# Chunked attention and a rational-activation feed-forward layer on one core: token blocks of 256 in place of 384, 256-column matmuls, attention in quarters, and an instruction order written out by hand

## The chip, the cores and the metric

The kernel runs on one core of a Trainium2 chip. The metric is the device time of one execution in microseconds (us), as the median of several executions. The core's engines each work through their own list of instructions, in order, and wait for one another on semaphores: TensorE (PE in the profile; PEld is its weight load), VectorE (DVE), ScalarE (ACT), GpSimd (POOL) and SyncE (SP), which here issues the DMAs. Matmuls write to PSUM, eight banks of 512 float32 columns; everything else lies in SBUF.

## The reference

Two stages, one behind the other. First attention inside chunks of 64 tokens: 8 batches, 8 heads, 576 tokens, head size 64, so 9 chunks for each head. Then a feed-forward layer over all 4608 tokens (d_model 512, d_ff 2048) with a rational function between its two matrices.

```
scores = scale * np.matmul(q_c, k_c.transpose(0, 1, 2, 4, 3))      # 64x64 per chunk and head
attn = np.exp(scores - np.max(scores, axis=-1, keepdims=True))
attn = attn / (np.sum(attn, axis=-1, keepdims=True) + 1e-09)
x = np.matmul(attn, v_c)                                          # then (4608, 512), heads side by side
h = x @ w_in                                                      # w_in 512 x 2048, float64
P = a[0] + a[1] * h + a[2] * h2 + a[3] * h3                       # h2 = h*h, h3 = h2*h
Q = 1.0 + np.abs(b[0]) * np.abs(h) + np.abs(b[1]) * h2
out = (P / (Q + 1e-6)) @ w_out                                    # w_out 2048 x 512, float64
```

The weights come as float64 and are rewritten to float32 on the chip. Both big products are made in three matmuls each, since the factors are split into a rounded part (hi) and a rest (lo): hi*hi, hi*lo and lo*hi.

## The kernel before

**Blocks and steps.** The 4608 tokens are cut into 12 blocks of 384 (`BT`), each of three units of 128 tokens. A block goes through d_ff in 8 steps of 256 (two slices of 128). A step is: the first product, FF1 (`ff1_mm`, L252): two slices of 12 matmuls of 384 columns, into one pair of PSUM banks `ph`, of which there is one; a chain of elementwise operations; and the second product, FF2 (`ff2_mm`, L334), which runs two steps later (`LAG`): 18 matmuls of 512 columns into three banks `po0` to `po2`, which gather over the 8 steps of a block. So a block has 192 FF1 matmuls of 384 columns and 144 FF2 matmuls of 512.

**The chain.** ACT copies `ph` to `h` in SBUF (L281), then makes A=|b0 h| (L282), B=h^2 (L283) and C=a3 h+a2 (L284) from `h`. DVE makes Q in B (L293) and the numerator in C (L294, L295). ACT makes 1/Q as exp(-ln Q) in A (L288, L289). DVE makes `ghi` (L303) and the rest `glo` (L304 to L306). All work on 128 x 768 values.

**Attention.** One unit is 128 tokens of all heads. `att_s` (S below) makes the scores with 8 matmuls whose moving operand `kbd` holds two chunks' keys in a block-diagonal form with zeros, so 64 stationary and 128 moving columns over all 128 rows (L172). DVE takes the maximum (L183), ACT the exponentials with their sums (L187, 8 instructions with a read of the accumulator each), DVE divides. `att_t` (T) transposes (L205), ACT copies the two halves to the block-diagonal `abd` (L208). `att_av` (AV) multiplies with v (L226), ACT and DVE split the result into `xhi` and `xlo` (L233, L238). The operands are float32, and the trace shows each such matmul as two, while a transposition is one. The units of the next block are spread over the steps of the present one.

**Weights.** 32 pieces of 128 x 512 are loaded and decoded (DVE L122, L124, L125, ACT L123, L126); the rest of a piece is made on DVE (L134) or, for half of the pieces, on TensorE with two products into PSUM (L130, L131) and a copy by ACT (L132).

**What sets the order.** The source is written step by step, and a planner with a model of the instructions' times orders each engine's list; only the last two steps are kept as they are written. `PROLOGUE` says what stands before the first FF1, and `DECODED` how many pieces are decoded by which step.

Of the kernel before, what the change touches and what calls it, by code (L numbers as in the profile page):

```python
# [38 lines left out]
def tile_chunked_attention_rational_moe(  # L39
# [30 lines left out]
    loaded = {}  # L70

    def load(u, qt=None, kt=None, vt=None, part="qkv"):
        if u >= NU:
            return
        if qt is None:
            qt = p2.tile([P, 512], F32, tag="qt", name=f"qt{u}", bufs=1)
            vt = p2.tile([P, 512], F32, tag="vt", name=f"vt{u}", bufs=1)
            kt = kbd
        loaded[u] = (qt, kt, vt)
        if "q" in part:  # L80
            load_qk(u)
        if "v" in part:
            load_v(u)

    def load_qk(u):
        qt, kt, vt = loaded[u]
        nc.sync.dma_start(out=qt, in_=qT[u])
        for par in range(2):
            rows = slice(64 * par, 64 * par + 64)
            nc.sync.dma_start(out=kt[rows, par, :], in_=kT[u, rows, :])  # L90

    def load_v(u):
        nc.sync.dma_start(out=loaded[u][2], in_=vP[u])

    def zero_rest(kt):
        nc.gpsimd.memset(kt[0:64, 1, :], 0.0)
        nc.gpsimd.memset(kt[64:128, 0, :], 0.0)

    def load_early(u):
        flat = lambda t: t.rearrange("p a b -> p (a b)")  # L100
        kt = p2.tile([P, NHP, BT], F32, tag=("xhi", "xlo")[u % 2], name=f"kt{u}")
        kt = flat(kt)[:, :1024].rearrange("p (a b) -> p a b", a=2)
        qt = p2.tile([P, 2, BT], F32, tag="A", name=f"qt{u}")
        vt = p2.tile([P, 2, BT], F32, tag="B", name=f"vt{u}")
        zero_rest(kt)
        load(u, flat(qt)[:, :512], kt, flat(vt)[:, :512], "q")
# [4 lines left out]
    raws = {}  # L111

    def piece_load(i, src):
        raw = p2.tile([P, 512, 2], I32, tag="raw", name=f"raw{i}", bufs=4)
        nc.sync.dma_start(out=raw, in_=src.rearrange("p (f w) -> p f w", w=2))
        raws[i] = raw

    def piece_decode(i, hi, lo):
        raw = raws.pop(i)
        low, high = raw[:, :, 0], raw[:, :, 1]  # L120
        val = high.bitcast(F32)
        nc.vector.tensor_scalar(low, low, 29, None, ALU.logical_shift_right)  # L122
        nc.scalar.activation(val, val, AF.Copy, scale=2.0 ** -111)  # L123
        nc.vector.scalar_tensor_tensor(low, high, 3, low, ALU.logical_shift_left, ALU.bitwise_or)  # L124
        nc.vector.scalar_tensor_tensor(high, high, -(2 ** 31), low, ALU.bitwise_and, ALU.bitwise_or)  # L125
        nc.scalar.activation(hi, val, AF.Copy, scale=2.0 ** -8)  # L126
        if i in LO_ON_PE:
            tag = ("pss", "pst", "psx")[i % 3]
            pl = ps_a.tile([P, 512], F32, tag=tag, name="pl")
            nc.tensor.matmul(pl, ident, val, start=True, stop=False)  # L130
            nc.tensor.matmul(pl, nident, hi, start=False, stop=True)  # L131
            nc.scalar.activation(lo, pl, AF.Copy, scale=2.0 ** -8)  # L132
        else:
            nc.vector.scalar_tensor_tensor(lo, val, 2.0 ** -8, hi.bitcast(F32), ALU.mult, ALU.subtract)  # L134

    def w_in_piece(fq, cc):
        f = slice(512 * fq, 512 * fq + 512)
        words = slice(1024 * fq, 1024 * fq + 1024)
        return w_in[cc * P:(cc + 1) * P, words], wi_hi[:, cc, f], wi_lo[:, cc, f]

    def w_out_piece(fc):
        return w_out[fc * P:(fc + 1) * P, :], wo_hi[:, fc, :], wo_lo[:, fc, :]

    make_identity(nc, ident)
    nident = cp.tile([P, P], F32R, tag="nident", name="nident")
    nc.vector.tensor_scalar_mul(nident, ident, -256.0)
    nc.gpsimd.memset(abd[0:64, 1, :], 0.0)
# [13 lines left out]
    ebuf = {}  # L161

    def att_s(u):
        qt, kt, vt = loaded[u]
        if u < UPB:
            pss = ps_o.tile([P, 512], F32, tag=f"po{u}", name=f"pss{u}")
        else:
            pss = ps_a.tile([P, 512], F32, tag="pss", name=f"pss{u}")
        for hp in range(NHP):
            for j in range(2):  # L170
                c0 = hp * 128 + j * 64
                nc.tensor.matmul(  # L172
                    pss[j * 64:(j + 1) * 64, hp * 128:(hp + 1) * 128],
                    qt[:, c0:c0 + 64],
                    kt[:, :, c0:c0 + 64],
                    start=True, stop=True,
                )
# [293 lines left out]
```

## Time and profile before

| | us |
|---|---|
| median of 3 executions | 974.58 (974.03 to 974.93) |
| span of the profiled execution, first to last instruction | 971.9 |
| what lies around the span, by that median | 2.7 |
| TensorE busy in it | 942.6 (97%) |
| weight loads busy | 816.3 (84%) |
| VectorE busy | 787.5 (81%) |
| ScalarE busy | 702.0 (72%) |
| first FF1 matmul starts at | 37.7 |

The profile is of one execution. A row of a timeline gives start and duration in us, the engine, the line of the source and the operation with its operands (what is written, an arrow, what is read: of a matmul first the moving, then the stationary operand), then shapes and a count. "128*64" is rows times columns of the array in use. A row of a group gives a count, the busy time, the mean duration in ns of one, and the idle time before them. Matmuls overlap in their pipeline, so the distance from one start to the next, and not the duration, tells what one costs in a stream.

### The profile page before, as it was taken

Reading aid. Unit: us, or ns where it says so; the run is one execution under the profiler, and the core shown is the slowest. Engines: PE = TensorE matmul, PEld = TensorE weight load, DVE = VectorE, ACT = ScalarE, POOL = GpSimd, SP = SyncE. Lnnn points to the kernel's source line nnn. Section 1 sums busy time; section 2 is a strip of 40 time slices with the busy share of each in tenths; the row PEclk is TensorE's granted clock in tenths of the full one; section 3 lists DMA queues with packets and bytes.
Section 4 is the critical chain, followed back from the end, with each engine's and each line's share of the span. In section 5 each row is a group of like instructions: output and inputs, shape, how many; then the busy total and the mean of one; then the engine's idle time right before and its main releaser. Section 6 shows DMA issues by size and latency. Waiting matters only on the chain.

```text
span 971.9 us, 14009 instructions
## 1 busy us (share of the span) xinstructions
PE 942.6 (97%) x5376; PEld 816.3 (84%) x5376; DVE 787.5 (81%) x1011; ACT 702.0 (72%) x1353; POOL 4.9 (1%) x16
## 2 busy tenths in 40 slices
PE   4599999999999999999999999999999999999998
PEld 3477788898888888888888888888888888888996
DVE  6799999878787887887887887877877878877786
ACT  4799889758667777667767767775876776775764
POOL 2000000000000000000000000000000000000000
PEclk9799999999999999999999999999999999999999
DMA  7644423002002112101101100110111211100000
GB/s 252 189 154 142 163 87 110 12 1 66 4 30 66 33 33 65 34 12 59 61 12 52 56 24 26 62 44 23 65 33 34 65 33 34 65 12 1 33 1 33
DMA packets 26274, 55.43 MB, mean 57 GB/s; under 512 B 3680, under 2 KB 3680, under 8 KB 26208
## 3 DMA queue, kind: packets, MB, share of 16 engines
q1 hardware_dynamic: 26208, 54.54, 17.7%
q8 instruction: 42, 0.69, 0.3%
q14 instruction: 24, 0.20, 0.1%
HBM read 45.09 MB, written 9.44 MB: 56 GB/s over the span
## 4 chain that ended last, share of the span: by engine, by line
PE 89%; DVE 4%; DMA 3%; ACT 3%; issue 1%; SPq 1%; DVEq 0%; ACTq 0%
PE po L334 40%; PE ph L252 39%; PE pss L172 4%; PE psx L226 3%; DMA raw<-in_w_in 2%; PE pst L205 1%; DMA raw<-in_w_out 1%; PE pl L130 1%; ACT e L187 1%; DVE raw L124 1%; ACT raw L123 0%; DVE raw L125 0%; DVE raw L122 0%; SPq L90 0%; DVE C L295 0%
## 5 line engine op out<-in xcount | busy, mean ns | idle before, releaser
L252 PE MATMUL ph<-xhi,wi_hi 128*128 128x384 f32 x760 | 260.0, 342 | 3.7 <-ACT h L281 3.0
L252 PE MATMUL ph<-xlo,wi_hi 128*128 128x384 f32 x760 | 256.9, 338 | 0.2 <-DVE xlo L238 0.2
L252 PE MATMUL ph<-xhi,wi_lo 128*128 128x384 f32 x760 | 256.6, 338 | 0.0
L334 PE MATMUL po<-wo_hi,ghi 128*128 128x512 f32 x570 | 227.3, 404 | 0.0
L334 PE MATMUL po<-wo_lo,ghi 128*128 128x512 f32 x570 | 222.8, 396 | 0.0
L281 ACT COPY h<-ph 128x768 f32<-128x768 f32 x95 | 76.1, 802 | 202.1 <-PE ph L252 199.3
L252 PEld LDWEIGHTS ph<-xhi,wi_hi 128*128 128x128 f32 x760 | 143.3, 189 | 14.1 <-ACT h L281 4.4
L293 DVE SCALAR_TENSOR_TENSOR B<-B,ab,A 128x768 f32<-128x768 f32 x95 | 96.6, 1017 | 67.7 <-ACT B L283 67.1
L334 PE MATMUL po<-wo_hi,glo 128*128 128x512 f32 x570 | 150.4, 397 | 0.0
L252 PEld LDWEIGHTS ph<-xlo,wi_hi 128*128 128x128 f32 x760 | 143.4, 189 | 3.9 <-DVE xlo L238 0.7
L252 PEld LDWEIGHTS ph<-xhi,wi_lo 128*128 128x128 f32 x760 | 143.4, 189 | 0.8 <-issue 0.5
L334 PEld LDWEIGHTS po<-wo_hi,ghi 128*128 128x128 f32 x570 | 107.0, 188 | 27.0 <-issue 5.3
L303 DVE SCALAR_TENSOR_TENSOR ghi<-C,ab,A 128x768 fp32r<-128x768 f32 x94 | 95.7, 1018 | 41.7 <-ACT A L289 35.6
L334 PEld LDWEIGHTS po<-wo_hi,glo 128*128 128x128 f32 x570 | 106.7, 188 | 26.3 <-issue 0.8
L334 PEld LDWEIGHTS po<-wo_lo,ghi 128*128 128x128 f32 x570 | 107.0, 188 | 21.5 <-issue 1.6
L288 ACT ACTIVATE A<-B,cst 128x768 f32<-128x768 f32 x95 | 89.6, 943 | 13.4 <-DVE B L293 13.0
L305 DVE SCALAR_TENSOR_TENSOR B<-C,ab,B 128x768 f32<-128x768 f32 x95 | 96.8, 1019 | 2.5
L295 DVE SCALAR_TENSOR_TENSOR C<-C,ab,h 128x768 f32<-128x768 f32 x95 | 96.6, 1017 | 1.9
L284 ACT ACTIVATE C<-h,ab 128x768 f32<-128x768 f32 x95 | 96.6, 1017 | 0.1
L306 DVE TENSOR_TENSOR glo<-B,A 128x768 fp32r<-128x768 f32 x94 | 89.9, 956 | 5.4
L294 DVE TENSOR_TENSOR C<-C,h 128x768 f32<-128x768 f32 x95 | 90.4, 952 | 3.8 <-ACT C L284 3.8
L304 DVE SCALAR_TENSOR_TENSOR B<-B,ghi 128x768 f32<-128x768 f32 x94 | 90.0, 957 | 2.5
(95 smaller groups left out, 993.4 us busy)
## 6 DMA issues: line engine op xcount, KB each, us to landing
qt<-in_qT SPq DMA_DIRECT2D x36, 256.0 KB, 2.9
vt<-in_vP SPq DMA_DIRECT2D x36, 256.0 KB, 2.8
out<-o SPq DMA_DIRECT2D x36, 256.0 KB, 2.2
kbd<-in_kT SPq DMA_DIRECT2D x68, 128.0 KB, 3.3
raw<-in_w_in SPq DMA_DIRECT2D x16, 512.0 KB, 4.8
raw<-in_w_out SPq DMA_DIRECT2D x16, 512.0 KB, 3.7
kt<-in_kT SPq DMA_DIRECT2D x4, 128.0 KB, 4.7
ab<-in_a SPq DMA_DIRECT2D x1, 2.0 KB, 2.5
```

Source lines behind the costliest of these rows:

```text
L252: nc.tensor.matmul(acc, w, x[:, cc, :], start=(k == 0), stop=(k == 11))
L281: yield nc.scalar.copy(h, ph[:, :, :BT])
L284: yield nc.scalar.activation(C, h, AF.Identity, bias=a2, scale=a3)
L288: nc.scalar.activation(A, B, AF.Ln, bias=cst[:, 0:1], scale=2.0 ** -KLN)
L293: yield nc.vector.scalar_tensor_tensor(B, B, b1a, A, ALU.mult, ALU.add)
L294: yield nc.vector.tensor_mul(C, C, h)
L295: yield nc.vector.scalar_tensor_tensor(C, C, a1, h, ALU.add, ALU.mult)
L303: yield nc.vector.scalar_tensor_tensor(ghi, C, a0, A, ALU.add, ALU.mult)
L304: yield nc.vector.scalar_tensor_tensor(B, B, CQ, ghi.bitcast(F32), ALU.add, ALU.mult)
L305: yield nc.vector.scalar_tensor_tensor(B, C, a0, B, ALU.add, ALU.subtract)
L306: yield nc.vector.tensor_mul(glo, B, A)
L334: nc.tensor.matmul(obuf[n][i], g[:, fi, i * 128:(i + 1) * 128], w[:, 2 * s + fi, :], start=(s == 0 and k == first[i]), stop=(s == NST - 1 ...
```

## The change

Nearly the whole body is rewritten; what is computed stays the same.

- **Sizes.** 18 blocks of 256 tokens. A block goes through d_ff in 4 steps of 512 (`FPS`, four slices). FF1 (`ff1`, L281) is 48 matmuls of 256 columns for each step. FF2 (`ff2`, L346) has 24 products for each step, each issued as two matmuls of 256 columns with the same weights, but for the first and the last one into a bank of a block, which stay at 512: two for each of a block's first and last step. The elementwise work is on 128 x 1024 values, 72 steps in place of 96.
- **PSUM.** Four pairs of banks: `p0` and `p1`, which FF1 uses in turns (after the first ten steps), `po` for FF2, `pa` for attention and the weights' rests. The copy `h` is gone: ACT makes A, B, C straight from PSUM (L287, L290, L294), and DVE reads it there too (L310, L314).
- **Attention** is made a block (256 tokens) at a time, in three stages at the block's steps 0, 1 and 2. `quarters` (L178) makes scores and the product with v from 64 x 64 pieces, 32 for each, which take the four quarters of the array in turn: the row half goes with the chunk and the column half with the batch of rows that is written, and the two row halves write to different banks. No block-diagonal copies and no zeros are left, and q, k and v come in loads of 128 x 1024.
- **Weights** come as 16 pieces of 2 x 128 x 512; the rest of 9 of them is made on TensorE (L163, L164), of 7 on DVE (L156).
- **Order.** `tc.manual_schedule()` keeps each engine's list as the source has it. The first 12 steps follow a string, `START`, in which each letter is an operation of one engine and the number a step, a piece or a block; the first two blocks take turns there, step by step, so that each group of weights serves two steps. From step 12 a loop writes the order out.
- **End.** The last two steps are no longer cut in halves.

```diff
-UPB = 3          # units of a token block
+UPB = 2
+FPS = 4
+START = (
+    "q0 w0 S0 v0 k0 M0 w1 U0 s0 o0 E0 j0 q1 n0 s1 o1 N0 w2 j1 T0 i0 K0 v1 i1 A0 h0 h1 r0 o2 X0 s2 Y0 r1 w3 l0 j2 "
+    "S1 i2 l1 w4 h2 M1 F0 s3 o3 U1 E1 j3 i3 o4 s4 r2 n1 N1 a0 j4 c0 w5 i4 b0 p0 l2 h4 Q0 T1 h3 d4 s5 o5 w6 P0 K1 "
...
+    def quarters(out_cols, tile_out, stat, mov):
+        for g in range(NQ):
+            for par in range(2):
+                for c in range(2):
+                    rows = slice(64 * c, 64 * c + 64)
+                    cols = slice(g * 128 + par * 64, g * 128 + par * 64 + 64)
+                    nc.tensor.matmul(
+                        tile_out[par * 64:(par + 1) * 64, c, out_cols(g)],
+                        stat[rows, cols], mov[rows, cols], start=True, stop=True,
+                    )
...
+        ph = bank_pair(tag, f"ph{n}_{s}").rearrange("p a (b t) -> p (a b) t", t=BT)
+        for fi in range(FPS):
+            f = slice((FPS * s + fi) * P, (FPS * s + fi + 1) * P)
...
+            for k, (w, x, cc) in enumerate(mm):
+                nc.tensor.matmul(ph[:, fi, :], w[:, cc, f], x[:, cc, :], start=(k == 0), stop=(k == len(mm) - 1))
...
-        yield nc.scalar.copy(h, ph[:, :, :BT])
-        yield nc.scalar.activation(A, h, AF.Abs, scale=b0)
+        nc.scalar.activation(ch[n, s][1], ch[n, s][0], AF.Abs, scale=b0)
...
+        mm = [(ghi, w, fi, i) for fi in range(FPS) for i in range(2) for w in (wo_hi, wo_lo)]
+        mm += [(glo, wo_hi, fi, i) for i in range(2) for fi in range(FPS)]
...
+            start, stop = s == 0 and k == first[i], s == NST - 1 and k == last[i]
+            for c in ([slice(0, DM)] if start or stop else [slice(0, 256), slice(256, DM)]):
+                nc.tensor.matmul(
+                    obuf[n][:, i, c], g[:, fi, i * 128:(i + 1) * 128], w[:, FPS * s + fi, c], start=start, stop=stop,
+                )
...
+    for g in range(FIRST, total + LAG):
+        n, s = steps[min(g, total - 1)]
+        m, stage = n + 1, s if n + 1 < NB and g < total else None
...
+        if g < total:
+            one("Fab", g)
+            if stage == 1:
+                one("nN", m)
+            one("cQ", g)
+            if stage == 0:
+                one("SMU", m)
+                load_qk(m + 1)
+            if stage == 2:
+                one("A", m)
+                load_v(m + 1)
+            one("IJpP", g)
+            if stage == 0:
+                one("E", m)
+            if stage == 2:
+                one("X", m)
+            one("gHRG", g)
+            if stage == 2:
+                one("Y", m)
+        back = steps[g - LAG]
+        one("Z", g - LAG)
+        if back[1] == NST - 1:
+            store(back[0], last=(back[0] == NB - 1))
+        if stage == 1:
+            one("TK", m)
```

In these strings F is FF1 and Z is FF2; a, b, c are ACT's A, B, C and I, J its ln and exp; Q, p, P, g, H, R, G are DVE's seven operations in the order L298, L310, L314, L319, L323, L327, L331. S, T, A are the three matmul groups of attention, M, U, n, N its DVE operations, E the exponentials, K, X, Y the copies and the rest. Of the weights, w loads, o, j, i are DVE's and s, h ACT's decoding, r is the rest on TensorE and l its copy, d the rest on DVE. q and v load, O stores.

On TensorE, in the middle of the program before: the end of FF2 of step 3, a transposition, FF1 of step 6 and, inside FF2 of step 4, the AV of a unit (`pst` and `psx` are attention's banks, `po` FF2's, the number behind `ph` and `ghi` is the step).

```order
L334 MATMUL po_2_4017<-wo_hi,glo_3_4139 128x512 x2
L205 MATMUL pst_4270<-ident,e_4176 128x128 x4
L334 MATMUL po_0_4015<-wo_hi,ghi_4_4241 128x512
L252 MATMUL ph_6_4277<-xhi_3318,wi_hi 128x384
L252 MATMUL ph_6_4277<-xlo_3319,wi_hi 128x384
...
L334 MATMUL po_0_4015<-wo_lo,ghi_4_4241 128x512
L334 MATMUL po_1_4016<-wo_hi,ghi_4_4241 128x512
L334 MATMUL po_1_4016<-wo_lo,ghi_4_4241 128x512
L226 MATMUL psx_4321<-abd,vt_4161 64x128 x8
L334 MATMUL po_2_4017<-wo_hi,ghi_4_4241 128x512
```

The same engine in the middle of the program after: the end of a block's FF2 (step 3), the transpositions of the next block, FF1 of step 2, the AV, FF2 of the next block's step 0 and FF1 of step 3.

```order
L346 MATMUL po_4075<-wo_hi,glo_3_4183 128x256 x6
L346 MATMUL po_4075<-wo_hi,glo_3_4183 128x512
L238 MATMUL pst_4527<-ident,e_4335 128x128 x8
L281 MATMUL ph_2_4538<-xhi_4065,wi_hi 128x256
L281 MATMUL ph_2_4538<-xlo_4066,wi_hi 128x256
...
L178 MATMUL psx_4594<-at_4536,v_4059 64x64 x32
L346 MATMUL po_4643<-wo_hi,ghi_0_4352 128x512
L346 MATMUL po_4643<-wo_lo,ghi_0_4352 128x256 x2
...
L346 MATMUL po_4643<-wo_hi,glo_0_4353 128x256 x16
L281 MATMUL ph_3_4690<-xhi_4065,wi_hi 128x256
```

FF1 and FF2 now follow each other whole, attention stands between them and no longer inside, and a block has one group each of scores, transpositions and AV, where 256 tokens had two of each.

On VectorE, the first instructions before (`raw` are pieces of weights, `sm` the maxima and sums, `pss` scores, `e` the exponentials):

```order
L183 TENSOR_REDUCE sm_137<-pss_128 128x8
L192 TENSOR_TENSOR e_138<-pss_128,sm_137 128x512
L122 TENSOR_SCALAR raw_108<-raw_108 128x512
L124 SCALAR_TENSOR_TENSOR raw_108<-raw_108 128x512
L183 TENSOR_REDUCE sm_155<-pss_146 128x8
L194 TENSOR_REDUCE sm_137<-e_138 128x8
L125 SCALAR_TENSOR_TENSOR raw_108<-raw_108 128x512
L192 TENSOR_TENSOR e_156<-pss_146,sm_155 128x512
```

And after, up to the rest of the first block's x, which FF1 reads:

```order
L204 TENSOR_TENSOR e_130<-pss_88,sm_126 128x2x8x64
L137 TENSOR_SCALAR raw_86<-raw_86 128x1024
L145 SCALAR_TENSOR_TENSOR raw_86<-raw_86 128x1024
L226 TENSOR_REDUCE sm_126<-e_130 128x16
...
L137 TENSOR_SCALAR raw_128<-raw_128 128x1024
L232 TENSOR_TENSOR e_130<-e_130,sm_126 128x2x8x64
L145 SCALAR_TENSOR_TENSOR raw_128<-raw_128 128x1024
L149 SCALAR_TENSOR_TENSOR raw_86<-raw_86 128x1024
L149 SCALAR_TENSOR_TENSOR raw_128<-raw_128 128x1024
L137 TENSOR_SCALAR raw_146<-raw_146 128x1024
L267 TENSOR_TENSOR xlo_206<-psx_164,xhi_205 128x2x4x128
```

Before the first FF1 there now stands one block of 256 tokens and two pieces of 1024 columns; before, it was three units and four pieces of 512, with parts of later ones between.

More of the change, by code (lines that the diff above doesn't have):

```diff
@@ L65, in tile_chunked_attention_rational_moe @@
     ident = cp.tile([P, P], F32, tag="ident", name="ident")
-    kbd = cp.tile([P, 2, 512], F32, tag="kbd", name="kbd")
-    abd = cp.tile([P, 2, 512], F32, tag="abd", name="abd")
+    nident = cp.tile([P, P], F32R, tag="nident", name="nident")
     ab = cp.tile([P, 8], F32, tag="ab", name="ab")
[L70 to L106, printed above, removed]
@@ L111, in tile_chunked_attention_rational_moe @@
[L111 to L147, printed above, removed]
@@ new lines, in load_v, with w_in_pieces, w_out_pieces @@
+    def load_v(n):
+        if n >= NB:
+            return
+        v = p2.tile([P, W], F32, tag="vt", name=f"v{n}")
+        nc.sync.dma_start(out=v, in_=vP[n])
+        loaded["v", n] = v
+    def w_in_pieces(fq):
+        f = slice(512 * fq, 512 * fq + 512)
+        words = slice(1024 * fq, 1024 * fq + 1024)
+        return [(w_in[c * P:(c + 2) * P, words], wi_hi[:, c:c + 2, f], wi_lo[:, c:c + 2, f]) for c in (0, 2)]
+    def w_out_pieces(fq):
+        return [(w_out[c * P:(c + 2) * P, :], wo_hi[:, c:c + 2, :], wo_lo[:, c:c + 2, :]) for c in (4 * fq, 4 * fq + 2)]
@@ L333, in ff2_mm @@
         for k, (g, w, fi, i) in enumerate(mm):
-            nc.tensor.matmul(
-                obuf[n][i], g[:, fi, i * 128:(i + 1) * 128], w[:, 2 * s + fi, :],
-                start=(s == 0 and k == first[i]), stop=(s == NST - 1 and k == last[i]),
-            )
-    def store(n):
-        for i in range(UPB):
-            o = p2.tile([P, DM], F32, tag="o", name=f"o{n}_{i}")
-            nc.scalar.copy(o, obuf[n][i])
-            r0 = n * BT + i * 128
-            nc.sync.dma_start(out=out[r0:r0 + 128, :], in_=o)
@@ new lines, in tile_chunked_attention_rational_moe, with ph_tag, po_tag, consts @@
+    steps = [(n, s) for s in range(NST) for n in (0, 1)] + [(n, s) for n in range(2, NB) for s in range(NST)]
+    def ph_tag(g):
+        return "p1" if g == 1 or (g >= 10 and g % 2 == 0) else "p0"
+    def po_tag(n):
+        return "p1" if n == 1 else "po"
+    make_identity(nc, ident)
+    nc.gpsimd.memset(cst[:, 0:1], CQ * 2.0 ** -KLN)
+    nc.gpsimd.memset(cst[:, 1:2], -KLN * math.log(2.0))
+    nc.vector.tensor_scalar_mul(nident, ident, -256.0)
+    def consts(_):
+        nc.sync.dma_start(out=ab[:, 0:4], in_=a.partition_broadcast(P))
+        nc.sync.dma_start(out=ab[:, 4:6], in_=b.partition_broadcast(P))
+        nc.scalar.activation(b1a, ab[:, 5:6], AF.Abs)
```

450 lines of the change are left out of this document (204 added, 246 removed), and 9 rows, old and new, of the table START.

## Prediction

> **What bounds the kernel now.** First the page: busy shares, the slices, the chain that ended last.
>
> ```profile
> PE 942.6 (97%) x5376; PEld 816.3 (84%) x5376; DVE 787.5 (81%) x1011; ACT 702.0 (72%) x1353; POOL 4.9 (1%) x16
> ...
> PE   4599999999999999999999999999999999999998
> ...
> PE 89%; DVE 4%; DMA 3%; ACT 3%; issue 1%; SPq 1%; DVEq 0%; ACTq 0%
> ```
>
> TensorE is full from the third slice (some 48 us) to the end, and 89% of the chain is its own. A busy PE need not be at its peak, so the second look is at the timeline of one step in the middle: the first and last of FF1's 24 matmuls, the first and last of FF2's 12 with `ghi`, its 6 with `glo`, and the restart behind attention.
>
> ```profile
> 502.83 0.34 PE L252 MATMUL ph<-xhi,wi_hi 128*128 128x384 f32 x1
> ...
> 506.82 0.34 PE L252 MATMUL ph<-xhi,wi_lo 128*128 128x384 f32 x1
> ...
> 507.00 0.39 PE L334 MATMUL po<-wo_hi,ghi 128*128 128x512 f32 x1
> ...
> 509.56 0.39 PE L334 MATMUL po<-wo_lo,ghi 128*128 128x512 f32 x1
> ...
> 509.79 1.56 PE L334 MATMUL po<-wo_hi,glo 128*128 128x512 f32 x6
> ```
>
> ```profile
> 511.86 0.19 PEld L252 LDWEIGHTS ph<-xhi,wi_hi 128*128 128x128 f32 x1 [0.17 <-ACT A L288]
> 511.86 0.44 PE L252 MATMUL ph<-xhi,wi_hi 128*128 128x384 f32 x1
> 511.97 0.19 PEld L252 LDWEIGHTS ph<-xlo,wi_hi 128*128 128x128 f32 x1
> 512.14 0.33 PE L252 MATMUL ph<-xlo,wi_hi 128*128 128x384 f32 x1
> ```
>
> A matmul of 384 columns costs (506.82 - 502.83)/23 = 0.1735 us, one of 512 (509.56 - 507.00)/11 = 0.2327. At the restart two weight loads start 0.11 apart with nothing else in the way: a load of 128 columns needs no more than that, and hides under the matmul before it. Third, a block's period, from the copies of `po` three blocks apart, and the share of each engine in 100 us.
>
> ```profile
> 605.75 1.05 ACT L342 COPY o<-po 128x512 f32<-128x512 f32 x2
> ...
> 834.55 1.05 ACT L342 COPY o<-po 128x512 f32<-128x512 f32 x2
> ```
>
> ```profile
> 500.00:600.00 100.00, 100.00 (x571) 87.30 (x570) 79.50 (x97) 70.94 (x141) 0.00 (x0) 1.00 0.13 40
> ```
>
> The period is (834.55 - 605.75)/3 = 76.27 us, of which 192 x 0.1735 + 144 x 0.2327 = 66.82 are the two products and 9.45 attention. DVE (79.5) and ACT (70.9) have room. So TensorE's stream is the bound, and what the change is worth is read from it. Fourth, the ends.
>
> ```profile
> 6.79 1.98 PE L172 MATMUL pss<-kbd,qt 128*64 128x128 f32 x16 [6.79 <-DMA kbd<-in_kT]
> 8.80 0.69 DVE L183 TENSOR_REDUCE sm<-pss 128x8 f32<-128x512 f32 x1 [5.72 <-PE pss L172]
> ...
> 37.70 0.44 PE L252 MATMUL ph<-xhi,wi_hi 128*128 128x384 f32 x1 [0.69 <-ACT xhi L233]
> ...
> 38.59 1.14 PE L130 MATMUL pl<-raw,ident 128*128 128x512 f32 x2 [0.45 <-PE ph L252]
> 39.28 0.68 PE L131 MATMUL pl<-wi_hi,nident 128*128 128x512 f32 x1
> ...
> 967.34 0.63 PE L334 MATMUL po<-wo_hi,glo 128*128 128x512 f32 x2
> ```
>
> FF1 starts at 37.7, the last FF2 ends at 968.0, 3.9 before the span does. One weight's rest on TensorE takes 39.28 + 0.68 - 38.59 = 1.37. Check of the view: 37.7 + 12 x 76.27 - 9.45 (the last block has no next attention) + 16 x 1.37 + 3.9 = 969.3 of 971.9; 2.6 are waits.
>
> **The change part by part.**
>
> *256 columns.* A block of 256 tokens has 192 FF1 matmuls of 256 and 96 FF2 products, 92 of them cut in two: 376 of 256 columns and 4 of 512. The trace has no such matmul. Upper end: the price by the column of the 384 one, 0.1735 x 256/384 = 0.1157. The line through both prices gives 0.1735 - (0.2327 - 0.1735) = 0.1143, since the longer ones cost more by the column. Lower end: the load, which is no longer hidden with room, 0.11 as shown (0.1085 by rounding). I take 0.111, nearer to the load's row, as there the matmul stops being the longer of the two. A block's products then cost 376 x 0.111 + 4 x 0.2327 = 42.67, against 66.82 x 2/3 = 44.55: 1.9 less for each of 18 blocks. A page of the Trainium skill, "TensorE: Matmul & The Clock Gate", section "Back-to-back issue gap", gives N/2.4 + 2.5 ns for a warm array; by it 256 columns cost 109 ns and the sum would be 13 us lower, but for 384 it gives 162.5 where the trace has 173.5.
>
> *Attention.* Two groups, taken from the timeline of TensorE alone:
>
> ```profile
> 492.82 0.60 PE L205 MATMUL pst<-ident,e 128*128 128x128 f32 x4
> 498.44 1.09 PE L226 MATMUL psx<-abd,vt 128*64 128x128 f32 x16
> ```
>
> ```profile
> L226 PE MATMUL psx<-abd,vt x16: 272/273/323, 498.4 to 499.3; 128*64 128x128 f32 x16
> ```
>
> The 16 of AV take 0.82 from first to last start (1.09 less the last one's own 0.27). Transpositions, as wide and with full weights, come 0.11 apart ((0.60 - 0.27)/3), so 16 in a row would need 1.76: two run side by side, on the two column halves. Now the rows are halved too; 256 tokens have 64 passes of 64 columns for each of S and AV, where they had 32 of 128. If four run at once, their 4 x 0.82 = 3.28 is halved; if only two, it stays; that a gain of more than half is out follows from the count of columns. Of 256 tokens' 6.30 (9.45 x 2/3) the rest is 8 x 0.11 for T and 2.14 for the changes between six groups, 0.36 each, and three groups go: 1.07. So attention costs 3.6 to 5.2; I take 4.2, nearer to four at once because the trace shows the halves that it has running together. "TensorEngine Tiling (Array Packing)", section "Key Properties", in the Trainium skill says that tiles load and multiply independently; by it the lower end would hold, 11 us less in all; no row here shows row halves.
>
> *The elementwise work.* One row of each kind, and the same at half the width from the last step:
>
> ```profile
> L293 DVE SCALAR_TENSOR_TENSOR B<-B,ab,A 128x768 f32<-128x768 f32 x95 | 96.6, 1017 | 67.7 <-ACT B L283 67.1
> ...
> L294 DVE TENSOR_TENSOR C<-C,h 128x768 f32<-128x768 f32 x95 | 90.4, 952 | 3.8 <-ACT C L284 3.8
> ...
> L288 ACT ACTIVATE A<-B,cst 128x768 f32<-128x768 f32 x95 | 89.6, 943 | 13.4 <-DVE B L293 13.0
> ...
> L187 ACT ACTIVATE e<-pss,sm 128x64 f32<-128x64 f32 x272 | 82.0, 323 | 1.0 <-DVE sm L185 0.9
> ...
> L183 DVE TENSOR_REDUCE sm<-pss 128x8 f32<-128x512 f32 x36 | 24.8, 688 | 22.4 <-PE pss L172 22.3
> ...
> L238 DVE TENSOR_TENSOR xlo<-psx,xhi 128x512 fp32r<-128x512 f32 x36 | 24.7, 685 | 1.7 <-ACT xhi L233 1.7
> ...
> L124 DVE SCALAR_TENSOR_TENSOR raw<-raw 128x512 int32<-128x512 int32 x32 | 22.1, 692 | 0.2 <-ACT raw L123 0.2
> ...
> L122 DVE TENSOR_SCALAR raw<-raw 128x512 int32<-128x512 int32 x32 | 13.7, 429 | 8.0 <-DMA raw<-in_w_in 4.5 <-DMA raw<-in_w_out 3.0 <-PE pl L131 0.4
> ...
> L293 DVE SCALAR_TENSOR_TENSOR B_end<-B_end,ab,A_end 128x384 f32<-128x384 f32 x2 | 1.2, 611 | 0.0
> ...
> L294 DVE TENSOR_TENSOR C_end<-C_end,h_end 128x384 f32<-128x384 f32 x2 | 1.1, 551 | 0.0
> ```
>
> DVE pays (1017 - 611)/384 = 1.06 ns a column, so at 1024 one kind takes 1.29 and the other 952 + 256 x 1.04 = 1.22; L238, which reads PSUM, is no slower than L183 beside it, so reading `h` there is put at nothing. Four of 1.29 and three of 1.22 with their gaps make 9.0 a step, and with 4.2 of attention 40 a block; ACT, at no more than 943 x 4/3 = 1.26 for each of five operations, 16 x 0.32 of exponentials and 3 of copies, some 33. TensorE's 46.9 covers both, so the copy `h` that goes is worth nothing, and DVE would be next late, 7 us a block further on. From an FF1's end its chain takes some 11 us in a row, and FF2 of that step starts two FF1 and two FF2, 21 us, later. A pair `ph` is free after L314, some 6 us, and wanted after 16. Stores wait on SP for ACT's copy with the next v behind them, which is wanted a block later. All at nothing. At the very end FF2 of steps 69 and 70 (10.7 us) covers the last chain until `ghi`; without that cover it would be 3 us.
>
> *The start.* FF1 now waits for less: from 8.8, DVE does M, U, n, N (1.22 each), two L137 (0.7, twice the 429 less the fixed part), five decodes (1.23) and small ones, 12 us, then ACT, TensorE (2.7) and ACT make the second piece's rest, 5 us, and the second piece lands late: 27 (25 to 31). Against that the first 12 steps hold all decoding on DVE: 12 x 9.0 + 16 x (0.7 + 2 x 1.23) + 7 x 1.23 + four blocks' attention, 19 = 186. With 8.8 before it and the gaps that the next rows show (the numbers behind the length are PE's, PEld's and DVE's busy time; 40.00 - 28.39 - 8.8 = 2.8, then 20.00 - 15.53 = 4.5), step 11 leaves DVE at 202.
>
> ```profile
> 0.00:40.00 40.00, 19.25 (x144) 15.15 (x144) 28.39 (x60) 23.61 (x68) 4.88 (x16) 0.87 0.72 226
> 40.00:60.00 20.00, 17.26 (x79) 14.89 (x80) 15.53 (x29) 17.23 (x36) 0.00 (x0) 0.91 0.55 180
> ```
>
> TensorE wants it at 27 + 25 x 48 x 0.111 (14 FF1, 11 FF2) + 7 x 2.74 of weights + 12.5 of attention = 192. So it waits 10 in the start (3 to 16).
>
> *Sum.* 27 + 18 x (42.67 + 4.2) = 843.7, less 5.4 of attention that stands before the first FF1, + 19.2 weights + 10 + 3.9 = 898.4 span, and 2.7 around it, as between the span of 971.9 and the median of 974.6: **901**.
>
> **Rivals.**
>
> *The price by the column stays* at 0.1157: 18 x 1.77 = 32 more, less 6 of waiting that goes: 927, and 945 with attention at 5.2. For it: 384 and 512 differ by only 1% by the column. Chance 0.2.
>
> *The written order starves TensorE.* No planner fills gaps; the first 12 steps wait 40 instead of 10: 931. For it: DVE at 186 of some 200 us there. Against: in the loop every wait above has 5 us to spare. Chance 0.12.
>
> *Slower: the load binds.* From a load's start to its matmul's start are 0.17 (511.97 to 512.14), just what a 384 matmul costs. If a load needs that, 256 columns cost 0.17 too: 18 x (376 x 0.17 + 0.93 + 4.2) + 47 = 1290. Against it are the two loads 0.11 apart and the transpositions. It decides from 0.123 a matmul, where the sum meets 974.6, that is 11% over my price. Chance 0.07. The same page's "Part 3: Packing small matmuls" says that a load overlaps running matmuls only when its rows differ. Then load and matmul would add up to 0.22 and the time be about 1630. The loads that start with the matmul before speak against it: 0.01.
>
> *No change*, with a matmul within 0.0003 of 0.123: 0.02.
>
> **How the numbers follow.** Forecast 0.58; faster is the sum of the first three, 0.90; same 0.02 (0.2%, some 2 us, is what a measurement of this kernel tells from no change), slower 0.08. Low: 0.1085, attention 3.6, more waiting: 880. High: 0.1157, attention 5.2, a start of 30 and 10 of waiting: 953. That leaves out the load rival and part of the starved one.
>
> **What would show it.** FF1 rows of 256 columns 0.111 apart; S and AV groups of 64 under 1.1 us from first to last start; a period of 47 us from store to store; DVE full and TensorE with gaps until some 200 us, none after; first FF1 near 27. Wrong it would be with matmuls over 0.123 apart, or with TensorE idle in the loop.

## The result and the profile after

| | before | after |
|---|---|---|
| median, us | 974.31 (973.00 to 974.93, 4 executions) | 936.25 (934.77 to 937.58, 4 executions) |
| ratio after/before, 95% interval | | 0.9614 (0.9600 to 0.9629) |
| span of the profiled execution | 971.9 | 934.9 |
| first FF1 matmul starts at | 37.7 | 30.8 |
| a period, for 256 tokens | 50.85 (76.27 x 2/3) | 47.87 |

Faster by 38 us, where 73 were forecast. First the page of the kernel after: busy shares, the slices of TensorE and its clock, the chain that ended last.

```profile
PE 895.0 (96%) x9342; PEld 868.4 (93%) x9342; DVE 754.1 (81%) x670; ACT 566.2 (61%) x1002; POOL 0.8 (0%) x8
...
PE   2888799999999999999999999999999999999997
...
PEclk9889899999999999999999999999999999999999
...
PE 89%; DVE 4%; DMA 3%; ACT 2%; issue 1%; SPq 0%; DVEq 0%; ACTq 0%
```

TensorE still carries the chain, 89% of it, but it is full only from the sixth slice (117 us) on, where it was full from the third before, and its clock is below full speed in three of the first five slices. Then the timeline of TensorE in one step of the loop: the second and the second-last matmul of an FF1, the 64 scores of a block, and FF2 behind them, its rows two matmuls each.

```profile
537.75 0.28 PE L281 MATMUL ph<-xlo,wi_hi 128*128 128x256 f32 x1
...
543.05 0.28 PE L281 MATMUL ph<-xlo,wi_hi 128*128 128x256 f32 x1
...
543.38 1.16 PE L178 MATMUL pss<-qk 64*64 64x64 f32 x64
544.47 0.50 PE L346 MATMUL po<-wo_hi,ghi 128*128 128x256 f32 x2
...
545.03 0.39 PE L346 MATMUL po<-wo_hi,ghi 128*128 128x256 f32 x2
...
547.98 0.39 PE L346 MATMUL po<-wo_lo,ghi 128*128 128x256 f32 x2
```

A matmul of 256 columns costs (543.05 - 537.75)/45 = 0.1178 us in this FF1 and (547.98 - 545.03)/26 = 0.1135 in this FF2: two prices, around the 0.1157 by the column and above the 0.111 that was taken. The 64 scores take 1.16 less the last one's own 0.22, 0.94 from first to last start. Third, the period from the copies of `po`, eleven blocks apart, and the shares of 100 us in the loop.

```profile
322.17 1.01 ACT L359 COPY o<-po 128x1024 f32<-128x1024 f32 x1
...
848.77 1.01 ACT L359 COPY o<-po 128x1024 f32<-128x1024 f32 x1
```

```profile
500.00:600.00 100.00, 100.00 (x1071) 98.80 (x1070) 81.75 (x74) 62.67 (x133) 0.00 (x0) 1.00 0.14 44
```

(848.77 - 322.17)/11 = 47.87. TensorE does not idle in the loop; the products at 0.1157 are 376 x 0.1157 + 4 x 0.2327 = 44.43 of it, and 3.44 is left for attention. The groups of the elementwise work, one that reads no `ph` and two that do:

```profile
L298 DVE SCALAR_TENSOR_TENSOR B<-B,ab,A 128x1024 f32<-128x1024 f32 x72 | 92.4, 1284 | 109.1 <-ACT B L290 109.1
...
L314 DVE SCALAR_TENSOR_TENSOR C<-C,ab,ph 128x1024 f32<-128x1024 f32 x72 | 92.2, 1280 | 3.2 <-ACT B L290 1.0
...
L310 DVE TENSOR_TENSOR C<-C,ph 128x1024 f32<-128x1024 f32 x72 | 87.5, 1215 | 7.9 <-ACT B L290 5.0
```

L314, which reads `ph` in PSUM, costs what L298 does: 1280 and 1284 ns. Last, the ends. The timeline has the first FF1 and the two longest waits of TensorE behind it; the windows have the two stretches with half the clock (the columns are length, PE's, PEld's, DVE's, ACT's and POOL's busy time with counts, the granted clock, DMA); then the last instructions.

```profile
30.82 0.39 PE L281 MATMUL ph<-xhi,wi_hi 128*128 128x256 f32 x1
...
48.87 2.07 PE L163 MATMUL pl<-raw,ident 128*128 128x512 f32 x2 [3.33 <-ACT at L243]
...
113.63 0.55 PE L281 MATMUL ph<-xhi,wi_hi 128*128 128x256 f32 x1 [4.54 <-DVE C L314]
```

```profile
39.80:53.50 13.70, 9.03 (x19) 4.08 (x17) 12.96 (x13) 10.06 (x10) 0.00 (x0) 0.50 0.47 154
111.50:118.30 6.80, 4.67 (x22) 4.70 (x23) 6.80 (x8) 2.85 (x4) 0.00 (x0) 0.50 0.43 154
```

```profile
927.76 1.11 PE L346 MATMUL po<-wo_hi,glo 128*128 128x256 f32 x7
...
928.90 0.58 ACT L356 COPY o<-po 128x512 f32<-128x512 f32 x1 [11.24 <-PE po L346]
929.51 2.39 SPq L362 DMA_DIRECT2D out<-o  x4
929.52 0.69 DVE L357 COPY o<-po 128x512 f32<-128x512 f32 x1 [6.46 <-ACT o L356]
```

By the prediction's own sum: 30.8 + 18 x 47.87 - 4.4 (the attention that stands before the first FF1, 5.4 x 3.44/4.2) + 19.2 + waits + 6.0 (934.9 less 928.9) = 934.9, so TensorE waits or runs slow for 21.6 us in the start, where 2.6 were lost before. The trace bears that out to within 1 us: behind the first FF1 TensorE's waits add up to 15.7 us, 9.0 of them ended by ACT and 6.7 by DVE, and the two stretches at half the clock cost some 7 us, half of the 9.03 + 4.67 that TensorE is busy in them. Against before, products gave 2.1 us, attention 51.5, the first FF1 6.9, the weights on TensorE 2.7. The start's waits took 19 back, the end 2, and 5 is that less attention now stands outside the blocks' sum: 37 in all.

### The profile page after: what moved, and what is told of

It reads as the page before. It is cut to its first block, busy times and chain, and to the rows that moved or that the text cites. A ratio compares the mean times of both kernels' runs of the same rounds, so it can differ in the third digit from the quotient of the medians.

```text
span 934.9 us, 21016 instructions
## 1 busy us (share of the span) xinstructions
PE 895.0 (96%) x9342; PEld 868.4 (93%) x9342; DVE 754.1 (81%) x670; ACT 566.2 (61%) x1002; POOL 0.8 (0%) x8
## 4 chain that ended last, share of the span: by engine, by line
PE 89%; DVE 4%; DMA 3%; ACT 2%; issue 1%; SPq 0%; DVEq 0%; ACTq 0%
PE po L346 41%; PE ph L281 41%; PE psx L178 2%; PE pss L178 2%; PE pst L238 2%; DMA raw<-in_w_out 1%; PE pl L163 1%; DMA ab<-in_b 1%; DVE raw L145 1%; DMA raw<-in_w_in 1%; DVE B L298 1%; DVE raw L149 1%; DVE C L314 1%; ACT e L218 1%; DVE C L310 0%
## 5 line engine op out<-in xcount | busy, mean ns | idle before, releaser
L281 PE MATMUL ph<-xhi,wi_hi 128*128 128x256 f32 x1152 | 324.5, 282 | 4.8 <-DVE C L314 4.8
L281 PE MATMUL ph<-xlo,wi_hi 128*128 128x256 f32 x1152 | 322.5, 280 | 0.7 <-DVE xlo L267 0.7
L281 PE MATMUL ph<-xhi,wi_lo 128*128 128x256 f32 x1152 | 322.3, 280 | 0.0
L287 ACT ACTIVATE A<-ph,ab 128x1024 f32<-128x1024 f32 x72 | 80.5, 1118 | 271.6 <-PE ph L281 268.9
L346 PE MATMUL po<-wo_hi,ghi 128*128 128x256 f32 (+1 forms) x1116 | 230.5, 285 | 0.0
L346 PE MATMUL po<-wo_lo,ghi 128*128 128x256 f32 x1152 | 227.2, 278 | 2.4 <-DVE wo_lo L156 1.2
L281 PEld LDWEIGHTS ph<-xhi,wi_hi 128*128 128x128 f32 x1152 | 219.8, 191 | 6.1 <-issue 5.0
L281 PEld LDWEIGHTS ph<-xlo,wi_hi 128*128 128x128 f32 x1152 | 217.5, 189 | 1.1 <-DVE xlo L267 0.9
L281 PEld LDWEIGHTS ph<-xhi,wi_lo 128*128 128x128 f32 x1152 | 217.4, 189 | 0.0
L346 PEld LDWEIGHTS po<-wo_lo,ghi 128*128 128x128 f32 x1152 | 177.4, 188 | 4.4 <-DVE wo_lo L156 1.4
L298 DVE SCALAR_TENSOR_TENSOR B<-B,ab,A 128x1024 f32<-128x1024 f32 x72 | 92.4, 1284 | 109.1 <-ACT B L290 109.1
L346 PEld LDWEIGHTS po<-wo_hi,ghi 128*128 128x128 f32 x1116 | 170.7, 188 | 3.0 <-issue 0.8
L346 PE MATMUL po<-wo_hi,glo 128*128 128x256 f32 (+1 forms) x1116 | 145.3, 282 | 0.0
L346 PEld LDWEIGHTS po<-wo_hi,glo 128*128 128x128 f32 x1116 | 135.7, 188 | 0.8
L319 DVE SCALAR_TENSOR_TENSOR ghi<-C,ab,A 128x1024 fp32r<-128x1024 f32 x72 | 92.4, 1284 | 9.8 <-ACT A L306 1.3
L314 DVE SCALAR_TENSOR_TENSOR C<-C,ab,ph 128x1024 f32<-128x1024 f32 x72 | 92.2, 1280 | 3.2 <-ACT B L290 1.0
L327 DVE SCALAR_TENSOR_TENSOR B<-C,ab,B 128x1024 f32<-128x1024 f32 x72 | 92.5, 1284 | 2.3
L310 DVE TENSOR_TENSOR C<-C,ph 128x1024 f32<-128x1024 f32 x72 | 87.5, 1215 | 7.9 <-ACT B L290 5.0
L331 DVE TENSOR_TENSOR glo<-B,A 128x1024 fp32r<-128x1024 f32 x72 | 88.1, 1224 | 6.6
L294 ACT ACTIVATE C<-ph,ab 128x1024 f32<-128x1024 f32 x72 | 87.3, 1212 | 7.9 <-PE ph L281 4.7
L323 DVE SCALAR_TENSOR_TENSOR B<-B,ghi 128x1024 f32<-128x1024 f32 x72 | 88.2, 1224 | 2.2
```

What stands on the lines that cost most here:

```text
L281: nc.tensor.matmul(ph[:, fi, :], w[:, cc, f], x[:, cc, :], start=(k == 0), stop=(k == len(mm) - 1))
L287: nc.scalar.activation(ch[n, s][1], ch[n, s][0], AF.Abs, scale=b0)
L294: nc.scalar.activation(ch[n, s][3], ch[n, s][0], AF.Identity, bias=a2, scale=a3)
L298: nc.vector.scalar_tensor_tensor(B, B, b1a, A, ALU.mult, ALU.add)
L310: nc.vector.tensor_mul(C, C, h)
L314: nc.vector.scalar_tensor_tensor(C, C, a1, h, ALU.add, ALU.mult)
```

## The experiments

Medians in us; each ratio is against the kernel before, run on the same chip beside it.

**The kernel after again.** Nothing is edited.

> The changed kernel unchanged, on the chip and in the rounds of the next three, as what they are compared with: 936 us (935 to 938).

936.43 (935.88 to 937.05), ratio 0.9615 (0.9600 to 0.9629). This is the measure for the other runs.

**FF2 in 512 columns.**

```diff
-            for c in ([slice(0, DM)] if start or stop else [slice(0, 256), slice(256, DM)]):
+            for c in [slice(0, DM)]:
```

> FF2 issued as 96 matmuls of 512 columns a block and no longer as halves of 256. Theory, by the changed kernel's trace (0.116 us for 256 columns, 0.2327 for 512): the price goes by the column, so 96 x 0.2327 = 22.34 stands against 184 x 0.116 + 4 x 0.2327 = 22.27 a block, 1 to 2 us more in all: 936 to 939. Rival, the step of the prediction: a matmul of 256 is cheaper by the column, and the split was worth 184 x (0.1163 - 0.111) = 1 us a block: 950 or more. Second rival, against the split: half as many instructions and weight loads keep TensorE's queue fuller: 930 or less.

937.09 (935.49 to 938.08), ratio 0.9620 (0.9604 to 0.9636): the theory, and not to be told from 936.43. Two matmuls of 256 cost what one of 512 does, though they load the same weights twice: the load is hidden at 256, and no part of a matmul's price is fixed there.

**Other widths.** FF2's cuts differ by step: 4 x 128, then 192 + 320, then 128 + 384.

```diff
-            for c in ([slice(0, DM)] if start or stop else [slice(0, 256), slice(256, DM)]):
+            cuts = {1: (0, 128, 256, 384, 512), 2: (0, 192, 512), 3: (0, 128, 512)}.get(s, (0, 256, 512))
+            for c in ([slice(0, DM)] if start or stop else [slice(x, y) for x, y in zip(cuts, cuts[1:])]):
```

> FF2's second step of each block is cut into four products of 128 columns, its third into 192 and 320, its others as they are. Theory (a product in this stream costs by its columns alone, 0.453 ns each, whatever the cut): 192 costs 0.087 us, 320 costs 0.145, and their sum is the 0.232 of 256 and 256; 128 costs 0.058 if a load of weights hides under so short a product, and the time stays near 936. Rival (a fixed part per product, or a floor set by the load of weights): 128 costs more than 0.058; at a floor of 0.11 the second step's FF2 takes about 48 x 4 x 0.05 / 2 = 5 us more per block and the time grows by some 50 to 90 us, to 990 to 1030.

1059.94, one execution, above the rival's 990 to 1030. Three pairs of rows of its timeline, a pair for each cut; a row holds four matmuls in the first pair, two in the others.

```profile
486.18 0.61 PE L347 MATMUL po<-wo_hi,ghi 128*128 128x128 f32 x4
...
488.41 0.61 PE L347 MATMUL po<-wo_lo,ghi 128*128 128x128 f32 x4
...
501.27 0.42 PE L347 MATMUL po<-wo_lo,ghi 128*128 128x192 f32 x2
...
502.81 0.42 PE L347 MATMUL po<-wo_lo,ghi 128*128 128x192 f32 x2
...
513.12 0.45 PE L347 MATMUL po<-wo_lo,ghi 128*128 128x128 f32 x2
...
514.84 0.45 PE L347 MATMUL po<-wo_lo,ghi 128*128 128x128 f32 x2
```

128 columns cost (488.41 - 486.18)/20 = 0.1115, as much as 256 nearly; 192 + 320 cost (502.81 - 501.27)/6 = 0.257, and 128 + 384 cost (514.84 - 513.12)/6 = 0.287. The theory failed at the narrow ones and the rival's floor is there. With a floor of 0.11 us and a price of 0.452 us for a thousand columns (0.1735/384) above it, the pairs come to 0.11 + 0.145 = 0.255 and 0.11 + 0.174 = 0.284, within 0.003 of what was measured. So the price is the larger of 0.11 and, to within some 2%, the price by the column, and 256 stands just above the corner, which by these two figures is at 243 columns. The extra per block, 24 x 4 x 0.1115 - 24 x 0.2314 = 5.1, 24 x 0.026 = 0.6 and 22 x 0.055 = 1.2, is 6.9, or 125 us in 18 blocks, and 936 + 125 = 1061, where 1059.94 was measured. That the floor is the weight load's is argued, from the loads 0.11 apart in the prediction; a matmul without a new load was not tried.

**Two quarters at a time.** Each pair of quarters is finished before the other starts.

```diff
-        for g in range(NQ):
-            for par in range(2):
-                for c in range(2):
+        for c in range(2):
+            for g in range(NQ):
+                for par in range(2):
```

> The attention's S and AV products are issued as one half of the array after the other: all eight products of the two quarters that share a half, then those of the other two, in place of four quarters in turn. Theory (the time that attention lost, from 6.3 us per block before to about 3.4 now, comes from four quarters at work at once): a group of 64 products takes about 1.8 us from its first start to its last in place of 0.94, the period grows by about 1.7 us, and the time by 18 x 1.7 = 31 us, to about 967. Rival (attention became shorter because its groups are fewer and longer per token, with fewer changes of the array's shape, and the quarters as such bring nothing): the group stays near 0.94 us and the time at 936.

960.19 (957.50 to 960.91), ratio 0.9851 (0.9830 to 0.9873). The group of AV and the copies of two blocks in its timeline:

```profile
327.32 0.99 ACT L359 COPY o<-po 128x1024 f32<-128x1024 f32 x1
...
530.23 1.91 PE L178 MATMUL psx<-at,v 64*64 64x64 f32 x64
...
868.66 0.99 ACT L359 COPY o<-po 128x1024 f32<-128x1024 f32 x1
```

The group takes 1.69 from first to last start where it took 0.94, the period (868.66 - 327.32)/11 = 49.21, 1.34 more, and 18 x 1.34 = 24 us are the difference in time. Theory: four quarters at once are worth 24 us, by 0.75 a group and not the 0.86 that was expected. Attention gained 51.5 us in all, and no run shows where the other half comes from. The prediction put 1.07 a block, or 19 us, down to three groups fewer to change to and from, which was not tried alone.

**The quarters in another order.**

```diff
-            for par in range(2):
-                for c in range(2):
+            for c in range(2):
+                for par in range(2):
```

> The four quarters are fed in another order within each round of four; nothing else moves. In the kernel after, each stream of 256-column products between two interruptions holds one of two pitches, 0.1133 or 0.1178 us, the same from block to block, 4.5 of 8 streams of a block at the higher one or so. Theory (the pitch is set by how a stream starts behind attention or behind another stream): the group of 64 stays at 0.94 us, but streams change their pitch, and the period moves by up to 0.9 us either way from 47.87, the time by up to 16 us. Rival (the pitch belongs to the step, by its buffers or by what other engines do then): period 47.87, time 936.

936.35 (935.74 to 937.00), ratio 0.9613 (0.9595 to 0.9631). The rival holds: the period is 47.87 again, and the FF1 and FF2 of a block have the same pitches step for step. What gives a step its pitch stays open.

**One pair of banks and the copy.** FF1 has one pair, and `h` is copied out of it to SBUF. To make room, v has one buffer, and its loads stand behind the products that read it in `START`.

```diff
         ch[n, s][1:3] = t("A", 2), t("B", 2)
+        h = t("h", 1)
+        nc.scalar.copy(h, ch[n, s][0])
+        ch[n, s][0] = h
...
-        return "p1" if g == 1 or (g >= 10 and g % 2 == 0) else "p0"
+        return "p1" if g == 1 else "p0"
```

> One pair of FF1 banks, copied to SBUF by ACT as the kernel before did; the chain reads the copy; v has one buffer in place of two (for the room), and its loads stand behind the product that frees it. Theory: the copy costs ACT 72 x 1.05 = 76 us, which has 39% of the span free, frees the banks 1.1 us after FF1, while FF2 runs 5.6 us before the next FF1: same time in the loop, up to 6 us more in the start, where the chain is waited for: 936 to 943. Rival: the doubled banks and the missing copy are a source of the gain: 955 or more.

939.93 (936.88 to 940.84), ratio 0.9645 (0.9627 to 0.9663). The period is 47.87; what is lost, some 3.5 us, is lost in the start, where TensorE's waits stand behind ACT and DVE and none behind a load of v. So in the loop one pair with the copy is as good as two pairs without it.

**One pair of banks and no copy.**

```diff
-        return "p1" if g == 1 or (g >= 10 and g % 2 == 0) else "p0"
+        return "p1" if g == 1 else "p0"
```

> One pair of FF1 banks, read without a copy. By the changed kernel's trace DVE's last read of them (L314) ends 6.0 us behind FF1 where FF2 of 5.55 stands between, so the next FF1 waits some 0.6 us at two of four steps, and nothing at the two where attention stands between: 1.2 to 1.6 a block, 20 to 27 in all: 956 to 963. Rival: the doubling is not needed even without a copy, since DVE moves forward: 936 to 940.

979.15 (976.80 to 982.30), ratio 1.0059 (1.0036 to 1.0081): slightly slower than before, and 42.7 slower than the kernel after, twice what was expected. FF1 waits for L314, the chain's last reader of `ph`, which its timeline shows at four places, the last one typical of the loop:

```profile
185.51 0.55 PE L281 MATMUL ph<-xhi,wi_hi 128*128 128x256 f32 x1 [7.85 <-DVE C L314]
...
204.54 0.55 PE L281 MATMUL ph<-xhi,wi_hi 128*128 128x256 f32 x1 [5.00 <-DVE C L314]
...
221.87 0.36 PE L281 MATMUL ph<-xhi,wi_hi 128*128 128x256 f32 x1 [4.13 <-DVE C L314]
...
518.53 0.36 PE L281 MATMUL ph<-xhi,wi_hi 128*128 128x256 f32 x1 [0.54 <-DVE C L314]
```

The loop pays 1.4 a block, the expected part (some 20 us). Three waits of 4 to 8 us in the one block behind `START`, 17 together, and a clock that is at 0.83 to 0.91 in windows of 20 us around them, are the other half. Either a copy or a second pair keeps TensorE fed; without both it waits.

**No decoding on VectorE.** Leaves out DVE's shifts and joins of the weights (L137, L145, L149), so the products are made with other numbers.

```diff
         for item in program.split():
+            if item[0] in "oji":
+                continue
```

> Leaves out all of VectorE's part in splitting the weights into their high and low parts, so the low parts are not the reference's; the loads, ScalarE's part and every product stay. Theory (the start lost its 21 us of TensorE waits to a VectorE that has the weights and the first two blocks' elementwise work at once): the waits between the first FF1 and 130 us shrink from about 15 us after the first FF1 to under 5, and the time falls by 10 to 20 us, to 916 to 926. Rival (the start waits for the weights' transfers, which three buffers for raw weights hold back): the waits remain, with transfers as what ends them, and the time falls by less than 5 us.

926.53 (925.89 to 928.26), ratio 0.9514 (0.9495 to 0.9533): 9.9 us less, just short of the theory's 10 to 20. The period is unchanged and the first FF1 starts at 29.2, so by the same sum the start's waits are 12.3 in place of 21.6. The wait of 4.54 at 113.63 shrinks to 0.85 (104.66 there), but the one for ACT's copy in the early start stays as it was:

```profile
46.09 2.08 PE L163 MATMUL pl<-raw,ident 128*128 128x512 f32 x2 [3.39 <-ACT at L243]
```

TensorE's waits behind the first FF1 add up to 11.2 in place of 15.7, not to the under 5 of the theory. About as much again came by the clock. In eight windows of 20 us from the start it is below full speed in the first of these two only, and in the second, where the kernel after has its second stretch at half, it is at 1.00:

```profile
40.00:60.00 20.00, 13.89 (x130) 10.02 (x131) 10.89 (x9) 14.31 (x15) 0.00 (x0) 0.83 0.48 159
...
100.00:120.00 20.00, 19.15 (x168) 18.97 (x167) 17.48 (x16) 12.22 (x12) 0.00 (x0) 1.00 0.44 155
```

At 0.83 over 20 us it is at half for 2 x 0.17 x 20 = 6.8 us, where it was for 20.5. So taking DVE's load away frees 9 of the start's 21.6 us, half of it from waits and half by the clock; of the 11.2 us of waits that are left, 9.7 are ended by ACT.

**The planner's order.**

```diff
-    ctx.enter_context(tc.manual_schedule())
```

> The same instructions, but the planner orders each engine's list again, with the source's order as its wish, as in the kernel before. Theory (TensorE alone sets the pace of a block, and its 44.4 us of products and 3.4 us of attention don't depend on the order; the order only decides what waits in the start): the period stays within 0.5 us of 47.87, the start changes by some us either way, and the time is 925 to 950. Rival (the written order is what keeps TensorE from waiting for the elementwise work of a step of 512): waits of TensorE for products' inputs appear in every block, 1 to 3 us each, and the time is 955 to 990.

945.12 (943.36 to 945.96), ratio 0.9700 (0.9684 to 0.9717). Its timeline has the copies of two blocks and one wait (its lines are numbered one lower):

```profile
124.48 0.55 PE L280 MATMUL ph<-xhi,wi_hi 128*128 128x256 f32 x1 [6.70 <-DVE C L313]
...
329.00 1.01 ACT L358 COPY o<-po 128x1024 f32<-128x1024 f32 x1
...
855.61 1.01 ACT L358 COPY o<-po 128x1024 f32<-128x1024 f32 x1
```

(855.61 - 329.00)/11 = 47.87, the same period to the hundredth, so the 8.7 us are lost in the start. The wait of 6.70 is not all new: its like in the written order took 4.54. In the profiled execution TensorE's waits behind the first FF1 add up to 18.6 in place of 15.7, and the clock, at 0.74, 0.83, 0.91 and 0.75 in four windows of 20 us, is at half for some 31 us in place of 20.5. The written order is worth 8.7 us of the 38, none of them in the loop.

**The low part of the first blocks on GpSimd**, with the end of the next run.

```diff
-        nc.vector.tensor_mul(gbuf[n, s][1], B, A)
+        (nc.gpsimd if n < 3 else nc.vector).tensor_mul(gbuf[n, s][1], B, A)
```

> The last elementwise step (the low part of the activation) of the first three blocks' twelve steps goes to GpSimd in place of VectorE, with the end of the kernel as in the run before with two output tiles. VectorE is spared 12 x 1.13 = 13.6 us of its work in the start, beside the 45 us that the run without the splitting of the weights left out for 9.7 us of time. Theory (VectorE's fullness holds the start back): the time falls by 9.7 x 13.6 / 45 = 3 us, to about 933, if GpSimd's multiplication, which no trace of this kernel shows yet, takes no longer than the 5.5 us that FF2's products with the high part cover. Rival (GpSimd's multiplication is so slow, or slows VectorE so much, that the low part comes late): TensorE's FF2 waits for it, and the time stays or rises by up to 10 us.

938.24 (938.10 to 938.48), ratio 0.9633 (0.9619 to 0.9647): the rival, 2.4 above the next run, which has the same end. GpSimd's multiplications in its timeline, the slowest and the fastest of twelve, and two of DVE's decodes beside them:

```profile
91.15 4.36 POOL L331 TENSOR_TENSOR glo<-B,A 128x1024 fp32r<-128x1024 f32 x1 [11.18 <-ACT wi_hi L152]
...
154.43 2.38 POOL L331 TENSOR_TENSOR glo<-B,A 128x1024 fp32r<-128x1024 f32 x1 [13.83 <-PE ph L281]
```

```profile
61.54 3.31 DVE L149 SCALAR_TENSOR_TENSOR raw<-raw 128x1024 int32<-128x1024 int32 x1
...
78.76 2.30 DVE L145 SCALAR_TENSOR_TENSOR raw<-raw 128x1024 int32<-128x1024 int32 x1
```

It needs 2.4 to 4.4 us where DVE needs 1.2, and these two of DVE's decodes take 3.31 and 2.30 in place of 1.22. DVE is spared 12 x 1.22 = 14.6 us, but its busy time falls by 3.9 only, from 753.8 in the next run to 749.9: most of what it is spared it loses to the neighbour. No wait of TensorE in the trace is ended by GpSimd.

**The end in two tiles.**

```diff
-            nc.scalar.copy(o[:, 0, :], po[:, 0, :])
-            nc.vector.tensor_copy(o[:, 1, :], po[:, 1, :])
...
+            copy, issue = (nc.scalar.copy, nc.vector.tensor_copy), (nc.sync, nc.scalar)
+            for c in range(2):
+                o = p2.tile([P, 2, DM], F32, tag="eo", name=f"o{n}_{c}")
+                copy[c](o[:, 0, :], po[:, c, :])
+                for u in range(UPB):
+                    issue[c].dma_start(out=rows[c, u], in_=o[64 * u:64 * u + 64, 0, :])
```

> The last block's output goes through two tiles, one for each half, so that VectorE's copy no longer waits for ScalarE's, and the second half's two stores are issued from ScalarE's queue beside the first half's on SyncE's. Theory (the end after the last FF2, 6.0 us, is two copies one behind the other and four issues in a row): the end shrinks to 3.5 to 4.5 us, and the time by 1.5 to 2.5 us, to about 934.5. Rival (the end is set by the landing of the last store alone): less than 0.5 us.

935.87 (934.38 to 938.11), ratio 0.9610 (0.9588 to 0.9631): the theory's 1.5 to 2.5 us did not come, and the run is not to be told from the kernel after. The last instructions:

```profile
928.59 0.58 ACT L358 COPY o<-po 128x512 f32<-128x512 f32 x1 [11.24 <-PE po L346]
929.20 1.11 SPq L360 DMA_DIRECT2D out<-o  x2
929.21 0.69 DVE L358 COPY o<-po 128x512 f32<-128x512 f32 x1 [6.46 <-ACT o L358]
929.93 1.31 ACTq L360 DMA_DIRECT2D out<-o  x2
```

DVE's copy still starts behind ACT's, with a tile of its own, so the shared output tile was not what held it; what does was not found. The stores' issue ends at 931.24 and not 931.90, and the end shrinks from 6.0 to 5.4.

## Why the prediction was right, and where it was not

- **What bounds the kernel** was right: TensorE's stream, before and after; every run that left it alone kept 47.87.
- **256 columns at 0.111** failed, and with it the largest term: 18 x (44.43 - 42.67) = 32 us. The step that failed is the choice "nearer to the load's row, as there the matmul stops being the longer of the two". Some 0.11 is a floor (128 columns cost 0.1115), but 256 columns take longer than it, so the columns set the price; two bounds were read as two ends of an estimate where the larger of the two holds. That the load makes the floor is argued; that there is a floor, and that 256 columns stand above it, is shown. The rival *the price by the column stays* is what happened. The Trainium skill's "TensorE: Matmul & The Clock Gate", section "Back-to-back issue gap", has a formula for the gap that gives an estimate of 109 ns for this width; the trace has 113 to 118, and the measurement decides.
- **Attention at 4.2** came out at 3.44, 14 us better in 18 blocks, just below the lower end. Four quarters do run at once (0.94 a group, 1.69 when two are fed at a time), where the middle was taken for want of a row. "TensorEngine Tiling (Array Packing)", section "Key Properties", in the Trainium skill, says that tiles load and multiply independently; with 1.69/0.94 = 1.8 between two and four at a time, where full independence would give 2, the trace nearly agrees.
- **The elementwise work at nothing** was right: reading `h` in PSUM costs nothing (1280 against 1284 ns), one pair with the copy and two without have the same period, and DVE has 18% to spare there. The row that the prediction rested this on doesn't show it, since L183 reads PSUM as L238 does; L197 does, all in SBUF, with 688 ns in the kernel before against L238's 685.
- **The start's waits at 10** were 21.6, outside the 3 to 16. DVE's fullness was the right place for 9.3 of them, about half of these by the clock. The step that failed is that everything else in the start was taken as covered: TensorE's list has the weights' rests and attention of the second block between the FF1, and there it waits for ACT (9.0 in all, 3.33 of it at 48.87); and the clock is at half in 20.5 us, in which TensorE is busy for 9.03 + 4.67, so some 7 us are lost to it (an estimate from those rows; no run separates it).
- **The first FF1 at 27** was 30.8, in the range. **The end at 3.9** was 6.0: without the cut of the last two steps two copies stand one behind the other and four issues in a row, 2.39 us; a second queue for two of these gave 0.6 back.
- **The sum.** The period is 47.87 against 46.87, 18.0 us; first FF1 3.8; waits 11.6; less attention before the first FF1 1.0; the end 2.1; around the span 1.35 in place of 2.7, -1.35: 35.2, the whole difference of 936.25 from 901. Two errors of 32 and 14 us cancelled in half, which was luck: had attention cost the 4.2 of the forecast, the time would have been some 950. (In the recorded sum, 843.7 is 18 x 46.87 alone; the 27 before it is counted in the 898.4.)
- **The rivals.** The load binds at 0.17, and the slower side with it: refuted by 0.1135 to 0.1178, and so is a load and a matmul one behind the other at 0.22: loads are busy for 98.80 of the 100 us in which the matmuls are for 100.00. That the written order starves TensorE: in the loop it does not, and in the start the planner's order loses 8.7 us more.

## What to carry to other kernels

In these streams, where each matmul has a new weight load, one costs the larger of two things, a floor (by the argument above, the load) and the columns, and not something between them: narrower moving operands bring nothing above that corner and cost much below it. Read every term of the start by the list of the engine that bounds the kernel, item by item, since a full second engine was less than half of what was lost there. When a pass over the data frees a buffer early, as the copy `h` did, taking it away must be paid for with a second buffer, though neither shows in the time by itself.

## What the runs showed of the hardware that was not expected

- The price of a matmul has a corner: 0.1115 us for 128 columns, 0.1135 to 0.1178 for 256, 0.1735 for 384, 0.2327 for 512.
- A stream of 256 columns holds one of two pitches, 0.1135 or 0.1178, the same in each block and in another order of the quarters; at the lower one throughout, a block would be about 0.8 us shorter (an estimate, 384 x (0.1157 - 0.1135)). What chooses it was not found.
- GpSimd's multiplication of 128 x 1024 took 2.38 to 4.36 us, and an instruction of VectorE beside it up to 3.31 in place of 1.22, though not every one is slowed.
- The granted clock fell to 0.50 in two stretches of the start, 13.7 and 6.8 us long, and nowhere else while TensorE works: (13.7 + 6.8) x 0.5/934.9 is the 0.011 by which the mean of 0.989 falls short. Waits of TensorE of over 3 us stand in the first and at the beginning of the second; what else it takes was not tried.
